# A written-out schedule changed: one state turned by a transfer, a new order and coarser pieces at the end

## The chip, the cores and the metric

The kernel runs on one core of one Trainium2 chip. The metric is device microseconds for one launch. Engines are called as in the profile: PE (matrix multiplications), PEld (its weight loads), DVE, ACT, POOL, and SP, which here only issues transfers. ACT and POOL issue transfers too.

## The reference, cut to what matters

For 8 batches and 8 heads, 512 tokens and 32 state rows of width 64 attend to each other in both directions. The results, 544 rows per batch with 512 columns, go through three products whose maximum is taken, and one more product:

```python
scores = scale * x @ state.T ; a = softmax(scores) ; xread = a @ state
scores2 = scale * state @ x.T ; a2 = softmax(scores2) ; sread = a2 @ x
x2 = concat([xread, sread], axis=2)            # (8, 8, 544, 64) -> (4352, 512)
h = maximum(maximum(x2 @ w1, x2 @ w2), x2 @ w3) # 512 -> 768
out = h @ w_out                                 # 768 -> 512, float32
```

## The kernel before

The kernel doesn't compute xread. For each batch it forms G = state times w1, w2 and w3 (`g_slice`, `g_run`), and layer 1 multiplies the turned weights aT by G (`layer1`, line 477). Layer 1 is done in six parts of 128 of the 768 columns; each part m fills three PSUM banks, one for each of the three weight matrices. ACT copies the first bank out (`max_first`, line 492), DVE takes the maximum with the second (`max_second`, 497) and with the third (`max_third`, 505). Layer 2 (`layer2`, 514) takes the 512 tokens of a batch in four groups j of 128 and accumulates over the six parts; ACT or DVE copies each result to `osb` (526), and a store sends it out. The 32 state rows of all 8 batches together make one more block "s" with 256 rows: layer 1 from `atp` and the weights (`layer1_states`), layer 2 in two groups.

At the end of the program, layer 2 of batch 7 and of block s is cut by columns: `layer2_part` (l2p, 532), `layer2_part_out` (l2pc, 537) and `store_part` (sop, 541 and 543) compute, copy and store the columns c0 to c1 of a group. `store_states` (sos, 556) stores a whole group of block s.

The states come in four tiles k, each for the batches 2k and 2k+1; state tile 3 serves batches 6 and 7. `states_cast` makes it bfloat16, `states_turn` (stt) turns it by four PE transposes (line 261), and `states_place` (stp, 271) spreads it into the block-diagonal tile `bd` by two copies. `states_turn_dma` (std, 265) is there too, unused: it turns a tile by one transfer that SP issues. The tokens of batches 2 to 7 are turned by transfers as well (`x_turn_dma`, xtd, 291), and so are the attention weights (`a_turn_dma`, atd, 366) and the state readings (`sread_turn`, srt, 410, placed by `sread_place`, ap, 415).

There is no scheduler. The string PLAN is a list of steps, performed in that order; each step puts its instructions at the end of its engine's queue, and engines run their queues in order, each waiting on semaphores for what it needs. The last letter of a step names the engine that copies (D, A, P) or the queue that issues a transfer (S, A, P). The strings BANKS, PAIRS and PLACES say which PSUM bank and which buffer each step takes. POOL multiplies the attention weights (`weights`, wt, 349), pads the tokens (`pad`, 375), and issues the loads of tokens (206, 201) and most stores (548).

The last steps are `hold` (one multiplication, line 591, and one DVE copy of it, 593) and `vl`: all engines read a flag (583) and branch (674) over a repeat of the work that is needed only if sums ran out of range. It isn't taken here. After it come the instructions with which the program ends (739).

Of the kernel before, what the change touches and what calls it, by code (L numbers as in the profile page):

```python
# [15 lines left out]


PLAN = """
    lst 0 A; lxu 0 0 S; zero; clr 0; clr 1; clr 2; clr 3; warm; lxg 0 1; busy 1; xones 1; ident; busy 1;
    lxg 1 0; busy 1; busy 1; stc 0 D; busy 1; busy 1; busy 1; busy 1; busy 1; lxg 1 1; stt 0; busy 1; busy 1;  # L20
    cxu 0 0 D; xt 0 0; stp 0 A; busy 1; xt 0 1; lw 0 2 1; lw 0 1 0; xtc 0 0 D; sc 0 0; xones 0; lw 0 2 2;
    xtc 0 1 D; busy 1; busy 1; sc 0 1; xt 1 0; ex 0 0; ex 0 1; lw 1 3 0; sum 0 0; sum 0 1; xtc 1 0 A; busy 1;
    busy 1; xt 1 1; sc 1 0; xtc 1 1 D; ex 1 0; busy 1; busy 1; sc 1 1; lw 2 3 2; wt 0 1 D; lw 2 3 1; lw 3 4 0;
# [11 lines left out]
    so 0 0 2 P; lx 4; m0 1 5; l2 0 2; ma 1 5; mb 1 5; stp 3 A; l2c 0 2 A; l2 1 0; gq 2 1024 1280; gr 3 0 512;
    gr 3 1792 2304; l2c 1 0 D; grc 3 1792 2304 D; gqc 2 1024 1280 A; grc 3 0 512 A; atd 2; sr 2; l2 1 1; srs 2;
    sc 3 -; l1 2 0; m0 2 0; ex 3 -; l2c 1 1 D; l2 1 3; ma 2 0; gq 3 1024 1280; so 0 2 4 P; gqc 3 1024 1280 A;
    l2c 1 3 A; gr 3 512 1024; gr 3 1280 1792; mb 2 0; sum 3 -; wt 3 - P; atd 3; xtd 4; srt 0; sr 3; srs 3;
    l1 2 1; m0 2 1; ma 2 1; l1 2 2; m0 2 2; mb 2 1; ma 2 2; l1 2 3; m0 2 3; mb 2 2; ma 2 3; l1 2 5; m0 2 5;
    mb 2 3; l2 1 2; grc 3 1280 1792 A; grc 3 512 1024 A; ma 2 5; mb 2 5; l2c 1 2 D; l1 2 4; so 1 2 4 P; m0 2 4;  # L40
    ma 2 4; lx 5; mb 2 4; so 1 0 2 P; pad 4; gr 4 1792 2304; gr 4 0 512; grc 4 1792 2304 AD; l2 2 0; l2 2 1;
    grc 4 0 512 D; l2c 2 0 A; l1 3 0; m0 3 0; sc 4 -; ex 4 -; xtd 5; l2c 2 1 D; l2 2 3; ma 3 0; gq 4 1024 1280;
    gr 4 1280 1792; gr 4 512 1024; mb 3 0; sr 4; gqc 4 1024 1280 A; sum 4 -; srs 4; l2c 2 3 A; l1 3 1; m0 3 1;
    ma 3 1; l1 3 2; m0 3 2; mb 3 1; ma 3 2; l1 3 3; m0 3 3; mb 3 2; ma 3 3; l1 3 5; wt 4 - P; m0 3 5; mb 3 3;
    l2 2 2; grc 4 1280 1792 A; grc 4 512 1024 A; ma 3 5; mb 3 5; l2c 2 2 D; l1 3 4; so 2 2 4 P; m0 3 4; ma 3 4;
    lx 6; mb 3 4; atd 4; srt 1; ap 0 A; so 2 0 2 P; pad 5; gr 5 1792 2304; gr 5 0 512; grc 5 1792 2304 AD;
    l2 3 0; l2 3 1; grc 5 0 512 D; l2c 3 0 A; l1 4 0; m0 4 0; sc 5 -; ex 5 -; xtd 6; l2c 3 1 D; l2 3 3; ma 4 0;
    gq 5 1024 1280; gr 5 1280 1792; gr 5 512 1024; mb 4 0; sr 5; gqc 5 1024 1280 A; sum 5 -; srs 5; l2c 3 3 A;
    l1 4 1; m0 4 1; ma 4 1; l1 4 2; m0 4 2; mb 4 1; ma 4 2; l1 4 3; m0 4 3; mb 4 2; ma 4 3; l1 4 5; wt 5 - P;
    m0 4 5; mb 4 3; l2 3 2; grc 5 1280 1792 A; grc 5 512 1024 A; ma 4 5; mb 4 5; l2c 3 2 D; l1 4 4; so 3 2 4 P;  # L50
    m0 4 4; ma 4 4; lx 7; mb 4 4; atd 5; srt 2; ap 1 A; so 3 0 2 P; pad 6; gr 6 1792 2304; gr 6 0 512;
    grc 6 1792 2304 AD; l2 4 0; l2 4 1; grc 6 0 512 D; l2c 4 0 A; l1 5 0; m0 5 0; sc 6 -; ex 6 -; xtd 7;
    l2c 4 1 D; l2 4 3; ma 5 0; gq 6 1024 1280; gr 6 1280 1792; gr 6 512 1024; mb 5 0; sr 6; gqc 6 1024 1280 A;
    sum 6 -; srs 6; l2c 4 3 A; l1 5 1; m0 5 1; ma 5 1; l1 5 2; m0 5 2; mb 5 1; ma 5 2; l1 5 3; m0 5 3; mb 5 2;
    ma 5 3; l1 5 5; wt 6 - P; m0 5 5; mb 5 3; l2 4 2; grc 6 1280 1792 A; grc 6 512 1024 A; ma 5 5; mb 5 5;
    l2c 4 2 D; l1 5 4; so 4 2 4 P; m0 5 4; ma 5 4; mb 5 4; atd 6; srt 3; ap 2 A; so 4 0 2 P; pad 7;
    gr 7 1792 2304; gr 7 0 512; grc 7 1792 2304 AD; l2 5 0; l2 5 1; grc 7 0 512 D; l2c 5 0 A; l1 6 0; m0 6 0;
    sc 7 -; ex 7 -; l2c 5 1 D; l2 5 3; ma 6 0; gq 7 1024 1280; gr 7 1280 1792; gr 7 512 1024; mb 6 0; sr 7;
    gqc 7 1024 1280 A; sum 7 -; srs 7; l2c 5 3 A; l1 6 1; m0 6 1; ma 6 1; l1 6 2; m0 6 2; mb 6 1; ma 6 2;
    l1 6 3; m0 6 3; mb 6 2; srt 4; ma 6 3; l1 6 5; wt 7 - P; m0 6 5; mb 6 3; l2 5 2; grc 7 1280 1792 A;  # L60
    grc 7 512 1024 A; ma 6 5; mb 6 5; l2c 5 2 D; l1 6 4; so 5 2 4 P; m0 6 4; ma 6 4; mb 6 4; atd 7; ap 3 A;
    ap 4 A; so 5 0 2 P; srt 6; l1 7 0; srt 7; m0 7 0; l2 6 0; ap 7 D; srt 5; ma 7 0; mb 7 0; l1 7 2; m0 7 2;
    ap 6 A; l2c 6 0 D; ma 7 2; l1 7 3; m0 7 3; ap 5 A; mb 7 2; ma 7 3; l1 7 4; m0 7 4; l2 6 1; l2c 6 1 A;
    ma 7 4; mb 7 4; l1s 0; m0 s 0; l2 6 2; l2c 6 2 A; look; ma s 0; mb s 0; so 6 2 3 S; mb 7 3; l1 7 1; m0 7 1;
    ma 7 1; l1s 2; m0 s 2; mb 7 1; ma s 2; l1 7 5; m0 7 5; mb s 2; ma 7 5; l1s 1; m0 s 1; ma s 1; so 6 0 1 S;
    mb 7 5; l1s 5; m0 s 5; l2p 7 2 384 512; ma s 5; mb s 1; mb s 5; l1s 3; m0 s 3; l2pc 7 2 384 512 A;
    l2p 7 0 384 512; l2p 7 3 256 512; sop 7 2 384 512 P; ma s 3; l2p 7 2 128 384; mb s 3; l2p 7 0 0 128;
    l2pc 7 0 0 128 A; l2pc 7 3 256 512 D; l2p 7 1 0 128; l2pc 7 0 384 512 D; l2p 7 3 0 256; flag;
    l2pc 7 1 0 128 A; l2pc 7 2 128 384 A; l1s 4; m0 s 4; l2 6 3; sop 7 0 0 128 P; ma s 4; sop 7 0 384 512 P;
    mb s 4; l2p s 0 256 512; so 6 1 2 P; l2 s 1; sop 7 3 256 512 A; l2c 6 3 D; l2p 7 2 0 128; sop 7 1 0 128 S;  # L70
    so 6 3 4 A; l2pc 7 3 0 256 D; l2p s 0 0 256; l2pc s 0 256 512 D; sop s 0 256 512 A; l2pc 7 2 0 128 A;
    l2p 7 1 128 384; sop 7 2 0 128 A; l2p 7 0 256 384; l2pc s 0 0 256 A; l2pc 7 1 128 384 A; l2c s 1 D;
# [671 lines left out]
```

## Time and profile before

| | us |
|---|---|
| median of 3 runs | 152.14 (152.1 to 152.29) |
| span of the profiled execution | 150.5 |
| last matrix multiplication of the work ends in it | 146.95 |
| PE busy | 145.1 (96% of the span) |
| DVE, ACT, POOL busy | 118.0, 83.2, 56.1 |

The granted TensorE clock is 1.000 in the profiled execution. The profile does not give that execution's own device time; the median of the runs is 1.64 us over its span. Queue rows (SPq, POOLq, ACTq) stand for what an engine's sequencer does: it issues transfers, waits, branches. They are not counted as busy. Times of PE in the chain of waits are cut at the next step's start, those of the timeline are not.

### The profile page before, as it was taken

What the parts mean: (1) busy time and instruction counts of PE and PEld (TensorE: products, weight loads), DVE (VectorE), ACT (ScalarE), POOL (GpSimd) and SP (SyncE); (2) the same over time, 40 slices, a digit from 0 to 9 for tenths busy, and PEclk for the clock granted to TensorE, in tenths of its full rate; (3) what the DMA queues carried; (4) which work ended last, traced back from release to release, by engine and by line L of the source; (5) the groups of instructions that cost most, each with busy time, mean ns of one, the idle gap of its engine ahead of it and who ended that gap; (6) DMA issues with size and microseconds to landing.
All of it is one profiled execution on the core that took longest, in us unless ns stands there. A gap on an engine that the chain in (4) does not pass through costs nothing.

```text
span 150.5 us, 3618 instructions
## 1 busy us (share of the span) xinstructions
PE 145.1 (96%) x1422; PEld 72.8 (48%) x1422; DVE 118.0 (78%) x202; ACT 83.2 (55%) x144; POOL 56.1 (37%) x78
## 2 busy tenths in 40 slices
PE   6998999999999999999999999999999999999991
PEld 2556443335444443444344434443444446689770
DVE  6488788999967899789978997899789888674443
ACT  3366888965654574457546764676466653332220
POOL 6996911090392507350735064506250200001500
PEclk9999999999999999999999999999999999999999
DMA  4999999949647996998399839983303340300555
GB/s 121 195 188 189 206 230 198 196 97 139 124 97 171 235 182 189 108 209 178 145 102 216 183 139 90 231 183 131 157 4 78 121 175 7 139 0 17 190 199 167
DMA packets 39108, 22.29 MB, mean 148 GB/s; under 512 B 23072, under 2 KB 36896, under 8 KB 39088
## 3 DMA queue, kind: packets, MB, share of 16 engines
q0 software_dynamic: 15872, 13.96, 49.3%
q1 hardware_dynamic: 21632, 6.69, 22.8%
q10 hardware_dynamic: 1584, 1.38, 3.2%
q8 instruction: 12, 0.20, 0.6%
q14 instruction: 8, 0.07, 0.2%
HBM read 15.20 MB, written 8.91 MB: 160 GB/s over the span
## 4 chain that ended last, share of the span: by engine, by line
PE 88%; DMA 5%; POOL 3%; issue 1%; DVE 1%; ACT 1%; POOLq 0%
PE pw L477 47%; PE po L514 25%; PE pg L427 6%; DMA w<-in_moe_w_dram 5%; PE po L532 4%; PE ps L305 2%; PE psr L391 2%; POOL w L217 1%; POOL x L206 1%; PE pgh L427 1%; ACT G L444 1%; PE pt L261 1%; DVE held L593 0%; PE idle L591 0%; PE pat L358 0%
## 5 line engine op out<-in xcount | busy, mean ns | idle before, releaser
L477 PE MATMUL pw<-aT,G 128*128 128x512 bf16 x288 | 66.7, 379 | 0.0
L492 ACT CAST t<-pw 128x512 bf16<-128x512 f32 (+1 forms) x54 | 30.5, 564 | 27.3 <-PE pw L477 26.4
L497 DVE TENSOR_TENSOR t<-t,pw 128x512 bf16<-128x512 bf16 (+1 forms) x54 | 35.3, 654 | 11.1 <-ACT t L492 8.9
L477 PEld LDWEIGHTS <-G 128*128 128x128 bf16 x288 | 27.1, 98 | 32.8 <-issue 2.1
L514 PE MATMUL po<-wout,ht 128*128 128x512 bf16 x168 | 39.7, 379 | 0.0
L505 DVE TENSOR_TENSOR ht<-t,pw 128x512 bf16<-128x512 bf16 x48 | 32.9, 686 | 4.5
L349 POOL TENSOR_TENSOR a<-e,rden 128x1024 bf16<-128x1024 bf16 (+1 forms) x9 | 14.6, 1622 | 27.2 <-ACT osb L526 11.1
L514 PEld LDWEIGHTS <-ht 128*128 128x128 bf16 x168 | 15.4, 98 | 19.0 <-issue 1.7
L548 POOL DMA_DIRECT2D out_dram<-osb x13 | 7.4, 571 | 27.5 <-ACT t L492 27.5
L466 ACT CAST G<-pg 128x1024 bf16<-128x1024 f32 (+1 forms) x17 | 14.7, 895 | 2.1 <-PE pg L427 2.1
L526 ACT COPY osb<-po 128x512 f32<-128x512 f32 x15 | 8.9, 592 | 9.1 <-PE po L514 9.1
L526 DVE COPY osb<-po 128x512 f32<-128x512 f32 x14 | 9.6, 688 | 3.9 <-PE po L514 3.8
L375 POOL COPY xp<-x 128x1024 bf16<-128x1024 bf16 x12 | 12.3, 1059 | 0.0
L313 ACT ACTIVATE e<-ps 128x1024 bf16<-128x1024 f32 (+1 forms) x10 | 8.5, 854 | 6.7 <-PE ps L305 6.7
L466 DVE CAST G<-pg 128x1024 bf16<-128x1024 f32 (+1 forms) x12 | 11.6, 995 | 0.0
L342 DVE TENSOR_REDUCE seen<-e 128x32 f32<-128x1024 bf16 (+1 forms) x10 | 10.0, 997 | 1.7 <-ACT e L313 1.7
L427 PE MATMUL pg<-w,bd 64*32 64x512 bf16 (+1 forms) x288 | 10.7, 362 | 0.4 <-DMA w<-in_moe_w_dram 0.2
L444 ACT CAST G<-pg 128x768 bf16<-128x768 f32 x10 | 8.0, 810 | 2.7 <-PE pg L427 2.5
L543 POOL DMA_DIRECT2D out_dram<-osb x4 | 2.2, 544 | 19.4 <-ACT osb L537 19.4
L249 PE MATMUL idle<-zero 128*128 128x512 bf16 x18 | 7.4, 506 | 1.8 <-DVE zero L225 1.3
L477 PE MATMUL pw<-atp,w 128*128 128x256 bf16 x72 | 8.7, 272 | 0.0
L217 POOL DMA_DIRECT2D w<-in_moe_w_dram x10 | 7.7, 782 | 0.0
(70 smaller groups left out, 112.1 us busy)
## 6 DMA issues: line engine op xcount, KB each, us to landing
out_dram<-osb POOLq DMA_DIRECT2D x12, 512.0 KB, 3.7
x<-in_x_dram POOLq DMA_DIRECT2D x4, 512.0 KB, 7.2
x<-in_x_dram POOLq DMA_DIRECT2D x7, 256.0 KB, 5.8
w<-in_moe_w_dram POOLq DMA_DIRECT2D x4, 256.0 KB, 7.5
w<-in_moe_w_dram POOLq DMA_DIRECT2D x2, 384.0 KB, 7.5
wout<-in_moe_w_out_dram POOLq DMA_DIRECT2D x1, 768.0 KB, 12.0
out_dram<-osb SPq DMA_DIRECT2D x3, 256.0 KB, 2.4
stf<-in_state_dram ACTq DMA_DIRECT2D x4, 128.0 KB, 5.3
```

The lines of the kernel that those rows point to most:

```text
L342: nc.vector.reduce_sum(out=den, in_=parity(e[b], g), axis=AX.X)
L349: times[c](out=parity(a[b], g).rearrange("p j g s n -> p j (g s) n"), in0=parity(e[b], g).rearrange("p j g s n -> p j (g s) n"), in1=rdens ...
L375: nc.gpsimd.tensor_copy(out=xp[b][:, :, :, g * (D + 1):g * (D + 1) + D], in_=v[:, g])
L427: nc.tensor.matmul(p(s, g), bd(b, 2 * s + g)[64 * g:64 * g + 64, g, :], f(w_sb[64 * g:64 * g + 64, s]), start=True, stop=True, tile_positi ...
L444: copier[c[g]](out=G[b][:, g:h, :, m * 128:m * 128 + 128], in_=p[:, g:h, 0:384].rearrange("p g (i f) -> p g i f", i=3))
L466: copier[c[g]](out=v[:, g:h], in_=p[:, g:h, 0:c1 - c0])
L477: nc.tensor.matmul(pw[i][:, 0:n], lhs(i, k), rhs(k), start=(k == 0), stop=(k == nk - 1))
L492: nc.scalar.copy(out=t0s[b, m][:, 0:n], in_=open_ps["l", b, m][0][:, 0:n])
L497: nc.vector.tensor_max(t1s[b, m][:, 0:n], t0s.pop((b, m))[:, 0:n], open_ps["l", b, m][1][:, 0:n])
L505: nc.vector.tensor_max(ht[b][:, m, :], t1s.pop((b, m))[:, 0:n], open_ps.pop(("l", b, m))[2][:, 0:n])
L514: nc.tensor.matmul(p, ht[b][:, m, tokens(b, j)], wout_sb[:, m, :], start=(m == 0), stop=(m == NM - 1))
L526: copier[c[i]](out=o[:, j, i * w:i * w + w], in_=p[:, i * w:i * w + w])
```

## The change

Only the four strings change: no function is edited. In the first 60 us, `stt 3` (four PE transposes) goes, and `std 3` comes; its placement moves from ACT to POOL. Steps of batches 2, 3 and 4 change their order, and a few copies change between ACT and DVE. From batch 5 on the order stays, up to the last part of batch 6. There, batch 7's parts of layer 1 and block s's are done in another order, and layer 2 of the end is cut otherwise: `l2p` steps go from 14 to 8 (with the one whole group of block s 9 pieces, where there were 15), `sop` from 14 to 8, and batch 6 is stored in two transfers where it took four.

```diff
-    mb 0 4; sc 2 -; ex 2 -; grc 2 512 1024 D; stp 2 AD; stc 3 D; mb 1 4; l2 0 3; l2 0 0; l2c 0 3 A; l2c 0 0 A;
-    sum 2 -; l2 0 1; ones; pad 2; lxg 3 0; lxg 3 1; wt 2 - P; stt 3; xtd 3; l2c 0 1 A; l1 1 5; pad 3;
...
+    1024 1280; gr 3 0 512; gr 3 1792 2304; so 0 2 4 P; gqc 2 1024 1280 A; l2c 1 0 A; grc 3 0 512 DA; sr 2; grc 3
...
+    m0 3 0; sc 4 -; ex 4 -; xtd 5; std 3; l2c 2 1 D; l2 2 3;
...
-    l2p 7 1 384 512; l2p 7 0 128 256; sop 7 3 0 256 S; sop 7 2 128 384 P; l2pc 7 0 256 384 D; sop 7 1 128 384 A;
-    l2pc 7 1 384 512 D; sop 7 1 384 512 A; l2pc 7 0 128 256 D; sop 7 0 128 256 A; sos 1 S; sop s 0 0 256 S;
-    sop 7 0 256 384 S; hold; vl;
...
+    512 A; l2p 7 0 0 128; l2p 7 1 384 512; sop s 0 0 512 S; l2pc 7 1 0 384 D; sop 7 1 0 384 S; l2pc 7 1 384 512
+    A; l2pc 7 0 256 512 D; l2pc 7 0 0 128 D; sop 7 0 256 512 S; sop 7 1 384 512 A; sos 1 P; sop 7 0 0 128 S;
+    hold; vl;
```

The end of POOL's queue, before and after. The three DMA rows L543 and L548 that go are the last stores that POOL issued (three of batch 7, one of batch 6, one of batch 7); L556 is the whole group 1 of block s (`sos 1`); the L415 copy is `ap 5`.

```order
 L548 DMA out_dram<-osb 128x1024 x2
-L543 DMA out_dram<-osb 128x128 x3
-L548 DMA out_dram<-osb 128x512
-L543 DMA out_dram<-osb 128x256
+L415 COPY atp<-ats 128x4x32
+L543 DMA out_dram<-osb 128x512
+L556 DMA out_dram<-osb 32x4x512
 L583 TENSOR_LOAD flag
```

POOL now ends on two stores of 256 KB, `sop 7 3 0 512` and `sos 1`, instead of five of 64 to 256 KB.

What stands ahead of those two stores on ACT, as the change has it. The rows are ACT's copies of `l2p 7 0 128 256`, `l2p 7 3 0 512`, `l2 s 1` and `l2p s 0 0 512`, the store of group 2, and the last copy with its store.

```order
L492 CAST t_2319<-pw_2310 128x512
L537 COPY osb<-po 128x128
L537 COPY osb<-po 128x512
L526 COPY osb<-po 128x512
L537 COPY osb<-po 128x512
L543 DMA out_dram<-osb 128x512
L537 COPY osb<-po 128x128
L543 DMA out_dram<-osb 128x128
L583 TENSOR_LOAD flag
```

The copy of group 1 of block s (L526) was DVE's before and stood late in its queue; now it is ACT's, directly behind the copy that the other POOL store waits for.

SP's queue in the middle: x_86 and x_87 are the tokens of batches 4 and 5, the aT rows are `atd 2`, `atd 3` and `atd 4`, and stT is the new transfer of state tile 3.

```order
 L291 DMA_TRANSPOSE xT<-x_85 128x16x128
-L366 DMA_TRANSPOSE aT<-a 128x8x128 x2
+L366 DMA_TRANSPOSE aT<-a 128x8x128
+L410 DMA_TRANSPOSE ats<-sr 128x128
+L366 DMA_TRANSPOSE aT<-a 128x8x128
 L291 DMA_TRANSPOSE xT<-x_86 128x16x128
-L410 DMA_TRANSPOSE ats<-sr 128x128
 L291 DMA_TRANSPOSE xT<-x_87 128x16x128
+L265 DMA_TRANSPOSE stT<-st 128x4x128
 L366 DMA_TRANSPOSE aT<-a 128x8x128
```

`srt 0` moves ahead of `atd 3`, and the new transfer stands between `xtd 5` and `atd 4`. On POOL the load of batch 5's tokens moves at the same time, from ahead of `pad 4` to behind it.

More of the change, by code (lines that the diff above doesn't have):

```diff
@@ L18 @@
 PLAN = """
[L19 to L23, printed above, removed]
@@ L34 @@
-    sum 2 -; l2 0 1; ones; pad 2; lxg 3 0; lxg 3 1; wt 2 - P; stt 3; xtd 3; l2c 0 1 A; l1 1 5; pad 3;
[L35 to L72, printed above, removed]
-    l2p 7 1 384 512; l2p 7 0 128 256; sop 7 3 0 256 S; sop 7 2 128 384 P; l2pc 7 0 256 384 D; sop 7 1 128 384 A;
@@ new lines @@
+    1 4; l2 0 3; stp 2 AD; stc 3 D; l2 0 0; l2c 0 3 A; l2c 0 0 A; ones; sum 2 -; lxg 3 0; lxg 3 1; wt 2 - P; xtd
+    3; l2 0 1; l2c 0 1 A; pad 3; l1 1 5; lx 4; m0 1 5; l2 0 2; ma 1 5; l2c 0 2 A; mb 1 5; l2 1 0; gq 2 1024
+    1280; gr 3 0 512; gr 3 1792 2304; so 0 2 4 P; gqc 2 1024 1280 A; l2c 1 0 A; grc 3 0 512 DA; sr 2; grc 3 1792
+    2304 D; l2 1 1; srs 2; atd 2; sc 3 -; srt 0; l1 2 0; m0 2 0; ex 3 -; l2c 1 1 D; so 0 0 2 P; l2 1 3; ma 2 0;
+    gr 3 1280 1792; gq 3 1024 1280; gqc 3 1024 1280 A; mb 2 0; gr 3 512 1024; sum 3 -; l2c 1 3 A; wt 3 - P; atd
@@ new lines @@
+    3; sr 3; l1 2 1; srs 3; m0 2 1; ma 2 1; l1 2 2; m0 2 2; mb 2 1; ma 2 2; l1 2 3; m0 2 3; mb 2 2; ma 2 3; l1 2
+    5; m0 2 5; mb 2 3; l2 1 2; grc 3 1280 1792 A; grc 3 512 1024 A; ma 2 5; mb 2 5; l2c 1 2 D; l1 2 4; m0 2 4;
+    ma 2 4; so 1 2 4 P; gr 4 1792 2304; mb 2 4; xtd 4; pad 4; grc 4 1792 2304 AD; gr 4 0 512; grc 4 0 512 D; l2
+    2 0; l2 2 1; lx 5; l2c 2 0 D; so 1 0 2 P; l1 3 0; m0 3 0; sc 4 -; ex 4 -; xtd 5; std 3; l2c 2 1 D; l2 2 3;
+    gq 4 1024 1280; ma 3 0; l2c 2 3 A; gr 4 1280 1792; gr 4 512 1024; mb 3 0; sr 4; gqc 4 1024 1280 A; sum 4 -;
@@ new lines @@
+    srs 4; l1 3 1; m0 3 1; ma 3 1; l1 3 2; m0 3 2; mb 3 1; ma 3 2; l1 3 3; m0 3 3; mb 3 2; ma 3 3; l1 3 5; wt 4
+    - P; m0 3 5; mb 3 3; l2 2 2; grc 4 1280 1792 A; grc 4 512 1024 A; ma 3 5; mb 3 5; l2c 2 2 D; l1 3 4; so 2 2
+    4 P; m0 3 4; ma 3 4; lx 6; mb 3 4; atd 4; srt 1; ap 0 A; so 2 0 2 P; pad 5; stp 3 P; gr 5 1792 2304; gr 5 0
+    512; grc 5 1792 2304 AD; l2 3 0; l2 3 1; grc 5 0 512 D; l2c 3 0 A; l1 4 0; m0 4 0; sc 5 -; ex 5 -; xtd 6;
+    l2c 3 1 D; l2 3 3; ma 4 0; gq 5 1024 1280; gr 5 1280 1792; gr 5 512 1024; mb 4 0; sr 5; gqc 5 1024 1280 A;
@@ new lines @@
+    sum 5 -; srs 5; l2c 3 3 A; l1 4 1; m0 4 1; ma 4 1; l1 4 2; m0 4 2; mb 4 1; ma 4 2; l1 4 3; m0 4 3; mb 4 2;
+    ma 4 3; l1 4 5; wt 5 - P; m0 4 5; mb 4 3; l2 3 2; grc 5 1280 1792 A; grc 5 512 1024 A; ma 4 5; mb 4 5; l2c 3
+    2 D; l1 4 4; so 3 2 4 P; m0 4 4; ma 4 4; lx 7; mb 4 4; atd 5; srt 2; ap 1 A; so 3 0 2 P; pad 6; gr 6 1792
+    2304; gr 6 0 512; grc 6 1792 2304 AD; l2 4 0; l2 4 1; grc 6 0 512 D; l2c 4 0 A; l1 5 0; m0 5 0; sc 6 -; ex 6
+    -; xtd 7; l2c 4 1 D; l2 4 3; ma 5 0; gq 6 1024 1280; gr 6 1280 1792; gr 6 512 1024; mb 5 0; sr 6; gqc 6 1024
@@ new lines @@
+    1280 A; sum 6 -; srs 6; l2c 4 3 A; l1 5 1; m0 5 1; ma 5 1; l1 5 2; m0 5 2; mb 5 1; ma 5 2; l1 5 3; m0 5 3;
+    mb 5 2; ma 5 3; l1 5 5; wt 6 - P; m0 5 5; mb 5 3; l2 4 2; grc 6 1280 1792 A; grc 6 512 1024 A; ma 5 5; mb 5
+    5; l2c 4 2 D; l1 5 4; so 4 2 4 P; m0 5 4; ma 5 4; mb 5 4; atd 6; srt 3; ap 2 A; so 4 0 2 P; pad 7; gr 7 1792
+    2304; gr 7 0 512; grc 7 1792 2304 AD; l2 5 0; l2 5 1; grc 7 0 512 D; l2c 5 0 A; l1 6 0; m0 6 0; sc 7 -; ex 7
+    -; l2c 5 1 D; l2 5 3; ma 6 0; gq 7 1024 1280; gr 7 1280 1792; gr 7 512 1024; mb 6 0; sr 7; gqc 7 1024 1280
@@ new lines @@
+    A; sum 7 -; srs 7; l2c 5 3 A; l1 6 1; m0 6 1; ma 6 1; l1 6 2; m0 6 2; mb 6 1; ma 6 2; l1 6 3; m0 6 3; mb 6
+    2; srt 4; ma 6 3; l1 6 5; wt 7 - P; m0 6 5; mb 6 3; l2 5 2; grc 7 1280 1792 A; grc 7 512 1024 A; ma 6 5; mb
+    6 5; l2c 5 2 D; l1 6 4; so 5 2 4 P; m0 6 4; ma 6 4; mb 6 4; atd 7; ap 3 A; ap 4 A; so 5 0 2 P; srt 6; l1 7
+    3; m0 7 3; ma 7 3; srt 7; mb 7 3; srt 5; l2 6 0; ap 6 A; l2c 6 0 A; l1 7 2; m0 7 2; ap 7 D; ma 7 2; mb 7 2;
+    l2 6 3; l1 7 4; l2c 6 3 D; ap 5 P; m0 7 4; ma 7 4; l1s 2; m0 s 2; mb 7 4; ma s 2; l1s 1; m0 s 1; ma s 1; mb
```

48 lines of the change are left out of this document (28 added, 20 removed), and 3 rows, old and new, of the table BANKS.

## The prediction

> **What bounds the kernel now.** I read the page's busy times, then the chain of waits in order of time.
>
> ```profile
> span 150.5 us, 3618 instructions
> 38.64 0.22 PE pt L261 x4
> 38.86 1.29 PE pw L477 x6
> ...
> 75.68 1.29 PE pw L477 x6
> ...
> 135.09 0.33 PE po L532 x6
> 135.43 1.31 PE pw L477 x12
> 136.74 2.97 PE po L532 x36
> ...
> 141.04 1.29 PE po L514 x6
> 142.34 0.66 PE po L532 x6
> 143.00 1.29 PE po L514 x6
> 144.29 2.67 PE po L532 x36
> 146.95 0.02 issue
> 146.98 0.30 DVE osb L537
> ```
>
> The reader is to see that one PE piece follows the other without a gap until 146.95. PE work that goes away there is time, if nothing new makes PE wait. But the span goes on for 3.5 us behind PE, and the chain doesn't say what ends it. So I read, line by line, the queue rows of the branch (674) and of the program's end (739), and the last transfers (issues with their time to landing, for windows around them).
>
> ```profile
> L674 POOLq EVENT_SEMAPHORE  x5: 17/42/43, 142.1 to 145.3; - x5
> L674 POOLq INC_SWDGE_SEM  x1: 967/967/967, 145.4 to 145.4; - x1
> L739 POOLq DRAIN  x3: 46/109/3247, 146.4 to 150.2; - x3
> L739 SPq DRAIN  x3: 7/7/13, 149.3 to 149.9; - x3
> L739 POOLq EVENT_SEMAPHORE  x4: 17/17/17, 149.7 to 150.4; - x4
> ```
>
> ```profile
> 140.91 0.54 POOL L543 DMA_DIRECT2D out_dram<-osb  x1
> out_dram<-osb POOLq DMA_DIRECT2D x1, 128.0 KB, 4.3
> 146.37 1.43 ACTq L543 DMA_DIRECT2D out_dram<-osb  x3
> out_dram<-osb ACTq DMA_DIRECT2D x3, 64.0 KB, 1.8
> ```
>
> Two chains end the program. **SP's**: the last of ACT's three stores is issued at about 147.4 (their 1.43 us end at 147.8, one issue is some 0.4), lands 1.8 later at 149.2, and SP is through its waits at 149.3. **POOL's**: its last store is issued at 140.91 and lands 4.3 later, at 145.2. POOL waits for that (its waits run to 145.3), then takes 0.97 for INC_SWDGE_SEM and 3.25 for the DRAIN that starts at 146.4, and so gets to 149.6. The joint end starts at 149.7, right behind POOL and 0.4 behind SP. So POOL's chain ends last, by a little: from its last landing, 0.2 + 0.97 + 3.25 = 4.4 us to 149.6, and 0.85 more to 150.5.
>
> **The change part by part.**
>
> *Transposes of state tile 3.* Four PE transposes leave the chain: 0.22 us (38.64). PE then comes 0.22 earlier to `l1 1 5`, whose first bank ACT must have emptied before `l2 0 2` may take it.
>
> ```profile
> 38.68 0.59 ACT L526 COPY osb<-po 128x512 f32<-128x512 f32 x1 [0.71 <-PE po L514]
> 39.33 0.59 ACT L492 CAST t<-pw 128x512 bf16<-128x512 f32 x1
> ```
>
> ACT's cast starts 0.06 us behind the copy since it waits for PE; if PE comes earlier, it follows the copy at once and ends at 39.26 + 0.59 = 39.85 at the latest. PE wants the bank at 38.86 + 1.29 - 0.22 = 39.93 by the chain's times, some 0.1 to 0.2 earlier by the timeline's. So up to 0.1 may be lost again. I count 0.2 of the 0.22; bounds 0 and 0.22.
>
> *The transfer in its place, and its placement.* `std 3` stands in SP's queue ahead of `atd 4`, which `l1 4 0` needs at 75.68. At the same time the load of batch 5's tokens goes behind `pad 4`.
>
> ```profile
> 57.94 0.91 POOL L201 DMA_DIRECT2D x<-in_x_dram  x1
> 59.42 2.05 POOL L375 COPY xp<-x 128x1024 bf16<-128x1024 bf16 x2
> x<-in_x_dram POOLq DMA_DIRECT2D x4, 512.0 KB, 7.2
> 65.24 3.47 SPq L291 DMA_TRANSPOSE xT<-x  x1
> 68.80 1.26 SPq L366 DMA_TRANSPOSE aT<-a  x1
> aT<-a SPq DMA_TRANSPOSE x6, 2.9
> ```
>
> Now the load comes about 2.1 us later, at 60.0; it lands at 67.2, `xtd 5` takes 3.5 of SP until 70.7, the state's transfer, half as large as an aT, at most 1.3 until 72.0, and aT of batch 4, 2.9 us from issue to landing, is there at 74.9. PE wants it at 75.5. I cost it at nothing; the cover is the 0.6 us that are left (3.9 before). The two copies into `bd`, of 512 elements a row, fall to POOL, for which the trace has none of this form; two of its padding copies, 1024 each, take 2.05, so I bound both by 0 and 2.1. They stand ahead of `wt 5`; POOL is idle for up to 3.8 us ahead of a `wt`, and `bd` is first read by `gr 6`, a batch later. Nothing.
>
> ```profile
> POOL a L349 <- ACT osb L526: 11.1, 3, 3.8
> ```
>
> *Batches 2 to 4 in another order, copies between ACT and DVE.* PE's row order is nearly the same; `wt 2` waits for the same sums. DVE gets 0.69 more where `l2c 2 0` comes to it, ACT as much less. Bounds: 0.1 lost where a bank comes free just in time, 0.1 gained. Nothing.
>
> *PE at the end.* The columns are the same, cut into fewer pieces. 128 columns take 0.33 in a piece alone, 512 take 1.29, 0.324 per 128. The runs of 1152 and 1024 columns took 2.97 and 2.67, where 2.91 and 2.59 would follow: 0.14 for 12 pieces. About half the pieces go: 0.07. DVE might fall behind in the new order:
>
> ```profile
> L497 DVE TENSOR_TENSOR t<-t,pw 128x512 bf16<-128x512 bf16 (+1 forms) x54 | 35.3, 654 | 11.1 <-ACT t L492 8.9 <-PE pw L477 2.0
> L505 DVE TENSOR_TENSOR ht<-t,pw 128x512 bf16<-128x512 bf16 x48 | 32.9, 686 | 4.5
> ```
>
> An l1 of 1.29 us brings DVE 0.65 + 0.69 = 1.34 us. Each one that is left stands next to a layer-2 group that ACT copies or to state parts of half the columns, where DVE catches up, so I count no new stall; bound 0.3 lost. PE then ends at 146.95 - 0.20 - 0.07 = 146.7.
>
> *The stores.* Behind `l2 s 1` PE does 2560 columns, 20 x 0.324 = 6.5; so it ends at 140.2, and `l2p 7 3 0 512`, 640 columns on, at 141.8. ACT copies that (0.59, to 142.4) and then group 1 of block s (0.59, to 143.0).
>
> ```profile
> 136.17 0.27 ACT L537 COPY osb<-po 128x128 f32<-128x128 f32 x1
> 136.74 0.55 POOL L543 DMA_DIRECT2D out_dram<-osb  x1 [17.34 <-ACT osb L537]
> L526 ACT COPY osb<-po 128x512 f32<-128x512 f32 x15 | 8.9, 592 | 9.1 <-PE po L514 9.1
> out_dram<-osb POOLq DMA_DIRECT2D x1, 64.0 KB, 2.0
> out_dram<-osb SPq DMA_DIRECT2D x1, 256.0 KB, 2.5
> out_dram<-osb POOLq DMA_DIRECT2D x1, 512.0 KB, 2.9
> out_dram<-osb POOLq DMA_DIRECT2D x1, 256.0 KB, 4.5
> out_dram<-osb ACTq DMA_DIRECT2D x1, 128.0 KB, 4.0
> out_dram<-osb POOLq DMA_DIRECT2D x1, 64.0 KB, 4.1
> ```
>
> POOL issues 0.3 behind the copy that it waits for (136.44 to 136.74) and takes 0.55 for an issue: `sop 7 3` at 142.7, `sos 1` at 143.3. When does it land? Two bounds: 2.0 us (64 KB from POOL) and 4.5 (256 KB from POOL at 140.4; what was issued beside it, 64 KB from POOL and 128 KB from ACT, took 4.1 and 4.0). Nearest are the same store from SP, 2.5, and 512 KB from POOL with nothing beside it, 2.9. I take 2.7: 146.0. Before it was 145.2. So POOL's chain moves by +0.8: 146.0 + 4.4 + 0.85 = 151.3 for the span.
>
> The Trainium skill, in "DMA: Bandwidth & Descriptors", section "Anatomy of one DMA — SWDGE (gpsimd) path", gives about 2.0 us and bytes / 436e3 us for a transfer of this queue. By it the store would land 2.6 us behind its issue, an estimate from the page, and the sum would be 0.1 less.
>
> *SP's chain* gets shorter: PE ends 0.27 earlier, and the last store is no longer the third of a row on one queue: DVE's last copy is for the piece before PE's last, and the last two stores go out on two queues. I take 0.4 (bounds 0.27 and 0.6): the last store at 147.0 instead of 147.4, the end of the chain at 148.9. That is worth nothing as long as POOL ends at 150.4.
>
> **Sum.** Span 150.5 + 0.8 = 151.3. The median lies 1.64 over the profiled span; so 152.14 + 0.8 = 152.9.
>
> **Rivals.**
>
> *POOL's tail isn't a fixed cost.* INC_SWDGE_SEM and the DRAIN stand in the trace once, and a wait could be in them that ends with the others, since POOL is done only 0.3 behind SP. Against it: the other DRAINs in the rows above last 0.007 to 0.109 us, this one follows an instruction that stands in the end only once, POOL has no transfer under way, and nothing lands within the 0.4 us before its end. If it's elastic, SP's chain decides and takes the 0.4 along: span 150.1, time 151.75, faster. It decides if POOL's tail shrinks by 1.5 us or more.
>
> The Trainium skill ("VectorE: DVE Perf Modes", section "The DRAIN you can't avoid") says that the DRAINs of a program's start and end are constant, about 12 ns, on all engines. By that rule POOL would be through at 146.4 and this rival's time would come; the trace doesn't agree, with 3247 ns in one of POOL's three.
>
> *The gain is eaten, and the store lands early.* If `sos 1` lands within 2.0 to 2.2 us, POOL's chain moves by 0.1 to 0.3 only: 152.2 to 152.4, no change that could be told.
>
> *SP is late for batch 4.* If the late load and the state's transfer together cost more than the 0.6 us of cover, PE stands still at `l1 4 0`. Everything behind moves, POOL's tail included. At a load of 8 us (0.8 more than now) that is 0.2 more, and 153.1.
>
> *The transposes weren't time.* If the 0.22 is lost again at a bank, all of the end moves 0.2 later: 153.1 with POOL's tail, 152.0 with an elastic one.
>
> **How the numbers follow.** A measurement of this kernel can tell 0.2%, 0.3 us, from no change. POOL's tail with the later store: 0.58. Elastic tail: 0.25, nearly all of it faster. Store lands early: 0.10. Late for batch 4, in whatever tail: 0.07. Slower: most of 0.58, and 0.03 to 0.05 of the last: 0.60. Faster: 0.26. Within: 0.14. The likeliest one's own range is from a landing after 2.3 us (+0.4: 152.5) to one after 3.6 us (+1.7: 153.8); the range with the elastic tail begins at 151.6. Time 152.9, range 151.6 to 153.8.
>
> **What would show it.** Right: the POOL row INC_SWDGE_SEM of 674 starts near 146.2 instead of 145.4, its DRAIN again takes near 3.2 us and ends behind SP's last DRAIN by more than a microsecond, PE's last piece ends at 146.6 to 146.8, the first piece behind 38.6 is layer 1. Wrong: the DRAIN gets shorter while its start comes later (elastic tail), a gap of PE near 75 (late aT), PE's last piece not earlier than 146.9, or a last POOL store that lands before 145.5.

## The result: 1.6% slower, three times the loss that was forecast

The changed kernel takes 154.75 us (median of 6 runs, 153.87 to 155.63), the kernel before 152.21 beside it (152.1 to 152.4): 1.016 times as long, 95% interval 1.0125 to 1.0196. The forecast was 152.9 in a range of 151.6 to 153.8. The direction was right, the size was not: +0.8 forecast, +2.5 measured. One run of a1 below took 171.07 us at a granted clock of 0.856, and the ratio of a1 leaves it out.

The chain of waits of the changed kernel, its last pieces (start, length, what):

```profile
core 0 of [0], span 152.1 us
...
142.80 3.63 PE po L532 x30
146.43 0.02 issue
```

PE's last piece ends at 146.43, and 5.7 us follow where the kernel before has 3.5 (146.95 to 150.5). So PE doesn't make the loss; the program's end does. The queue rows of the branch (674) and of the end (739), each with its shortest, median and longest duration in ns and its first and last start:

```profile
L674 POOLq EVENT_SEMAPHORE  x5: 17/43/2312, 144.6 to 147.2; - x5
L674 POOLq INC_SWDGE_SEM  x1: 907/907/907, 147.3 to 147.3; - x1
```

```profile
L739 POOLq DRAIN  x3: 46/109/3002, 148.2 to 151.8; - x3
L739 SPq DRAIN  x3: 7/7/13, 149.9 to 151.5; - x3
```

POOL waits 2.3 us for its last transfer, until 147.1, and then takes 0.91 and 3.00: it is through at 151.24, 1.4 behind SP's first DRAIN (149.85). That is the chain of the forecast. What it waits for is `sos 1`; first the row of its issue in the timeline, then the landing in the view of line 556:

```profile
142.95 0.57 POOL L556 DMA_DIRECT2D out_dram<-osb  x1
```

```profile
DMA to landing us min/median/max: 4.1/4.1/4.1
```

4.1 us, where 2.7 was forecast. By the trace's landing events 15 of its 16 parts were there after 2.42 to 2.58 us, the last one after 4.10. In the window from 144.6 to 145.0 the transfer queues show one packet that is no data:

```profile
q8 instruction: 1, 0.02, 14.6%
```

It starts at 144.62 and moves 16 KB of instructions; such a transfer, by which an engine gets its next instructions, is called a **fetch** below. The four late stores of the kernel before (4.0 to 4.5 us) look the same: the POOL stores issued at 140.38 and 140.91 had 15 parts down within 2.54 and 2.58 us and the last after 4.48 and 4.26, with such a packet at 141.41. Its row, in the window from 141 to 143 of the kernel before:

```profile
q8 instruction: 1, 0.02, 4.5%
```

In the middle nothing was lost, as forecast: the state's transfer and aT of batch 4 follow `xtd 5` on SP, the latter is issued at 70.47 and lands at 73.20 (forecast 72.0 and 74.9; the load of batch 5's tokens landed at 65.87, not at 67.2), and PE comes to `l1 4 0` at 75.00 without a gap. SP's rows of the timeline, then the chain:

```profile
65.94 3.11 SPq L291 DMA_TRANSPOSE xT<-x  x1
69.10 1.26 SPq L265 DMA_TRANSPOSE stT<-st  x1
70.47 1.24 SPq L366 DMA_TRANSPOSE aT<-a  x1
```

```profile
72.30 2.70 PE po L514 x12
75.00 1.29 PE pw L477 x6
```

Near the end of the program a new stall appeared. The chain of the changed kernel at the first part of batch 7, `l1 7 3`, and of the kernel before at its first, `l1 7 0`:

```profile
116.21 0.45 PE pw L477 x2
116.65 0.02 issue
116.67 0.59 ACT t L492
117.27 0.02 issue
117.29 0.70 DVE t L497
117.99 0.04 issue
118.03 1.02 PE pw L477 x4
```

```profile
116.88 2.59 PE pw L477 x12
```

Before, 12 multiplications in a row took 2.59; now the same 12, from 116.21 to 119.06, take 2.85, since PE waits for ACT and DVE to empty a bank of `l1 6 4`. Every kernel of this study with the new end has this stall in its chain, and none with the old end.

### The profile page after: what moved, and what is told of

Read it like the earlier page. It is cut to its first block, busy times and chain, and to the rows that moved or that the text cites. A ratio compares the mean times of both kernels' runs of the same rounds, so it can differ in the third digit from the quotient of the medians.

```text
span 152.1 us, 3520 instructions
## 1 busy us (share of the span) xinstructions
PE 144.4 (95%) x1382; PEld 69.9 (46%) x1382; DVE 117.8 (77%) x199; ACT 81.4 (54%) x139; POOL 57.1 (38%) x78
## 4 chain that ended last, share of the span: by engine, by line
PE 86%; DMA 5%; POOL 2%; issue 1%; ACT 1%; DVE 1%; POOLq 0%
PE pw L477 46%; PE po L514 25%; PE pg L427 6%; DMA w<-in_moe_w_dram 5%; PE po L532 4%; PE ps L305 2%; PE psr L391 2%; POOL w L217 1%; POOL x L206 1%; PE pgh L427 1%; ACT G L444 1%; DVE t L497 0%; DVE held L593 0%; ACT t L492 0%; PE pt L261 0%
## 5 line engine op out<-in xcount | busy, mean ns | idle before, releaser
L548 POOL DMA_DIRECT2D out_dram<-osb x12 | 6.8, 569 | 27.0 <-ACT t L492 21.5
L466 ACT CAST G<-pg 128x1024 bf16<-128x1024 f32 (+1 forms) x17 | 14.2, 871 | 2.1 <-PE pg L427 2.1
L466 DVE CAST G<-pg 128x1024 bf16<-128x1024 f32 (+1 forms) x13 | 12.2, 973 | 1.8 <-PE pg L427 1.8
L526 ACT COPY osb<-po 128x512 f32<-128x512 f32 x16 | 9.5, 592 | 7.5 <-PE po L514 7.5
L526 DVE COPY osb<-po 128x512 f32<-128x512 f32 x13 | 8.8, 687 | 0.9 <-PE po L514 0.9
L543 POOL DMA_DIRECT2D out_dram<-osb x1 | 0.5, 545 | 23.2 <-ACT osb L537 23.2
L249 PE MATMUL idle<-zero 128*128 128x512 bf16 x18 | 6.9, 472 | 1.7 <-DVE zero L225 1.3
L477 PEld LDWEIGHTS <-w 128*128 128x128 bf16 x72 | 7.0, 98 | 1.5
```

The source lines that it names most:

```text
L466: copier[c[g]](out=v[:, g:h], in_=p[:, g:h, 0:c1 - c0])
L477: nc.tensor.matmul(pw[i][:, 0:n], lhs(i, k), rhs(k), start=(k == 0), stop=(k == nk - 1))
L526: copier[c[i]](out=o[:, j, i * w:i * w + w], in_=p[:, i * w:i * w + w])
```

## The experiments

The theory to test, A: the end is POOL's, from the landing of its last store, and the fetch of instructions makes that landing late. Two rivals: B, the new order and the larger pieces are slow on whatever queue; C, the loss is in the middle. Each run is compared with runs of the kernel before on the same chip, whose medians were 151.98 to 152.35. One measure is free of what the head and PE do in one execution: the time in the profile from the end of PE's last piece to the end of the span. It is called **the end** below; 3.5 us before, 5.7 in the changed kernel.

### Each part alone, and the whole again

e3 joins the plan of the change up to `mb 6 4` with the end of before, e4 the plan of before with the end of the change:

```diff
 e3:  ... l1 6 4; so 5 2 4 P; m0 6 4; ma 6 4; mb 6 4;          (as changed)
      atd 7; ap 3 A; ap 4 A; so 5 0 2 P; srt 6; l1 7 0; ...    (as before)
 e4:  the other way round
```

> The first part of the change alone: state tile 3 turned by a transfer and the new order of batches 2 to 4, with the end of the kernel before from atd 7 on. Theory A: 151.9 to 152.2 (0 to 0.2 faster than before), since the four transposes are 0.22 us of PE and the end is POOL's, with the landing of its last store. Rival C (the transfer or the late load of batch 5's tokens costs in the middle): 0.3 or more slower than before.

> The second part alone: the middle of the kernel before, and from atd 7 on the end of the changed one. Theories A and B: 153.5 to 155, the whole of the loss. Rival C: within 0.5 us of before.

> The changed kernel once more, unedited. Its profiled execution (153.87) was the fastest of six; the median was 154.75. Theory A with two more collisions: an execution near the median has POOL's tail later (sos 1 landing after more than 4.1 us), or the aT of batch 2 held by a fetch (landing 4.3 to 4.5 instead of 2.7, PE 0.8 to 1.1 later from 44.7 on). If neither, something else makes the other 0.9 us.

Measured: e3 154.75, 1.015 times before (1.012 to 1.019); e4 154.89, 1.017 (1.012 to 1.023); e12 154.4, 1.016 (1.012 to 1.020). e4 and e12 are theory A again: ends of 6.1 and 5.6 us, `sos 1` landing after 4.5 and 4.0, with fetches at 144.3 and 144.9. e12's aT of batch 2 came after 2.73, so the second collision that its expectation names was not in it. But e3 was a miss for all theories: it is as slow as the whole change, and although it changes only the first part, its loss sits at the end of the program. Its rows of the branch and of the end:

```profile
L674 DVEq COMPARE_BRANCH  x1: 84/84/84, 148.5 to 148.5; - x1
L674 DVEq EVENT_SEMAPHORE  x1: 21/21/21, 151.7 to 151.7; - x1
```

```profile
L739 SPq EVENT_SEMAPHORE  x14: 17/28/3345, 147.8 to 152.7; - x14
```

DVE stands 3.1 us behind its branch, and SP waits 3.3 us for DVE. In the kernel before DVE goes on 0.5 behind the branch. Up to there e3 had won 0.1 us: from the first layer-1 piece to PE's last piece 131.1 us, against 131.2 before and in the changed kernel, and 131.4 in e4.

e8 is e3 with six tiny DVE writes more in the head:

```diff
-        nc.vector.memset(bds[k], 0.0)
+        [nc.vector.memset(v, 0.0) for v in [bds[k]] + [bds[k][:, 0, 0, 0, 0:1]] * (6 * (k == 3))]
```

> The kernel of e3_middle_alone (first part of the change alone, which came out at 154.75) with six tiny DVE writes (one column each) added in the head. In e3 DVE stood 3.08 us behind its branch at 148.53 where it stands 0.48 in the kernel before, and SP waited 3.3 us for it. Theory: that stall depends on where DVE's instruction stream lies when the branch comes, so six more instructions ahead of it take it away: 151.9 to 152.3, as was expected of e3. If the stall comes from the first part's own work (a late copy or load): it stays at 154.5 or more, with 3 us behind DVE's branch.

Measured: 151.87 against 152.14, ratio 0.9993 (0.9968 to 1.0017), and the stall is gone:

```profile
L674 DVEq COMPARE_BRANCH  x1: 84/84/84, 147.8 to 147.8; - x1
L674 DVEq EVENT_SEMAPHORE  x1: 21/21/21, 148.4 to 148.4; - x1
```

So the first part costs nothing, as forecast, and rival C falls. The stall goes with the number of DVE's instructions: all three kernels of this study whose trace has 325 of them had it (e3, k2, k3: 3.06 to 3.31 us), none with 320, 321, 324 or 331 had. That the place of the instructions decides is argued from this and from e8. What happens in those 3 us no run shows: in e3 three packets of instructions come behind the branch, the last is done at 150.3, and DVE stands for 1.4 us more in which the traced transfers are still; the kernel before has three such packets there, too, and no stall. The Trainium skill, in "Runtime: NRT & Kernel Launch", section "Instruction fetch mechanics", says that a taken branch to a place outside the pages at hand must wait for a fetch; a stall of 3.1 us behind a branch fits that, but 1.4 of it have no fetch beside them.

### The two stores of POOL

e1 takes both from POOL, a1 only `sos 1`; b1 puts `sos 1` alone on POOL in the kernel before:

```diff
 e1:
-sop 7 3 0 512 P; ... sos 1 P;
+sop 7 3 0 512 S; sos 1 S; ...
 a1:
-sop 7 3 0 512 P; ... sos 1 P;
+sop 7 3 0 512 P; sos 1 S; ...
 b1, in the kernel before:
-sos 1 S;
+sos 1 P;
```

> The changed kernel with its last two POOL stores (sop 7 3 and sos 1) issued by SP instead, sos 1 directly behind sop 7 3; nothing else. Theory A (POOL's tail ends the program: last landing of a POOL store, then about 3.9 to 4.2 us of INC_SWDGE_SEM and DRAIN, then 0.85): POOL is done early, SP's chain ends last at about 149.9 as it does in the changed kernel, span 150.5 to 150.8, time 152.1 to 152.6, 2 us faster than the changed kernel's 154.75. Theory B (the order and the larger pieces at the end are slow by themselves, whichever queue issues): stays at 154 or more. If INC_SWDGE_SEM and DRAIN are a fixed cost, they last 0.9 and 3.0 to 3.3 us here too, only earlier; if the DRAIN is a wait for something that ends with the program, it ends with SP's again.

> The changed kernel with that one store, sos 1, issued by SP; sop 7 3 stays on POOL. Theory A: POOL's last landing is sop 7 3 (2.4 to 2.7 behind its issue at 142.4, so at 145.0), POOL is through at about 149.3, and SP's chain, 0.7 late by the fetch, ends at about 150.0 as in e1: 4.2 to 4.3 us from PE's last piece to the end, as e1's 152.9. If both POOL stores are needed for the loss of the changed kernel or the fetch now holds sop 7 3: 4.5 to 5.7, 153.3 to 154.5.

> The kernel before with one letter changed: sos 1 issued by POOL instead of SP. Theory A: POOL issues it at about 145.1, it lands 2.5 to 2.8 later (147.6 to 147.9; the fetch at 141.4 is past), INC_SWDGE_SEM and DRAIN take 4.2, 0.85 more: from the end of PE's last piece to the end of the span 5.9 to 6.2 us instead of 3.5, time 2.3 to 2.7 slower than before. If POOL's tail were elastic: within 0.3 of before.

Measured: e1 152.9 (152.1 to 152.6 expected), 1.0045 times before (1.0019 to 1.0072); a1 153.21, 1.0062 (1.0034 to 1.0089); b1 153.58, 1.0091 (1.0061 to 1.0121). e1 takes 1.8 us of the loss away (1.016 to 1.0045): theory B falls. The end is 4.2 us, SP's. POOL's rows in e1:

```profile
L674 POOLq INC_SWDGE_SEM  x1: 867/867/867, 145.1 to 145.1; - x1
```

```profile
L739 POOLq DRAIN  x3: 46/109/2839, 146.0 to 150.6; - x3
L739 SPq DRAIN  x3: 7/7/13, 150.0 to 150.3; - x3
```

POOL's DRAIN lasts 2.84 us here too and is over at 148.8, 1.2 before SP: it waits for nobody, so the rival of an elastic tail falls. The Trainium skill's statement that the DRAINs of a program's end are constant, about 12 ns, on all engines ("VectorE: DVE Perf Modes", section "The DRAIN you can't avoid") agrees with SP's 7 to 13 ns here, and not with POOL's 46 to 2839. a1 misses its 4.2 to 4.3 by little (4.5, where its expectation began the case that the loss needs both stores): POOL was through at 149.0, and SP's last stores took 2.7 to 3.3 us to land behind a fetch at 145.6.

b1 was a miss. Its end is 4.5, not 5.9 to 6.2, although `sos 1` landed even later than expected, at 149.3 instead of 147.6 to 147.9 (issued at 146.4 instead of 145.1, 2.9 us to land with no fetch near):

```profile
L674 POOLq INC_SWDGE_SEM  x1: 351/351/351, 149.4 to 149.4; - x1
```

```profile
L739 POOLq DRAIN  x3: 46/109/716, 149.8 to 151.4; - x3
```

0.35 and 0.72 us, where 0.97 and 3.25 stood before. SP's chain ended last here; why its last stores were late (2.9 to 3.4 us) the trace doesn't settle.

### What sets POOL's end

Over the profiles, POOL's long DRAIN, the first of its three, goes with the number of transfers that POOL issued in the whole program: 34 (e1) 2.84, 35 (a1) 2.92, 36 (changed) 3.00, 37 (e11) 3.08, 39 (before) 3.25. That is 0.0816 us each and 0.065 once. b1 has 40, and 0.72 is what that line gives for 8. k1 to k3 change the number, by cutting some of POOL's earlier stores in two:

```diff
 k1, in the changed kernel, for b = 2, 3, 4, 5; k2, in the kernel before, for b = 5:
-so b 0 2 P;
+so b 0 1 P; so b 1 2 P;
 k3, in the kernel before:
-so 5 2 4 P; ... so 5 0 2 P;
+so 5 2 3 P; so 5 3 4 P; ... so 5 0 1 P; so 5 1 2 P;
```

> The changed kernel (36 POOL transfers) with four earlier POOL stores (the first halves of batches 2 to 5) cut into two each, so that POOL issues 40. Theory N (the number sets POOL's end, and at 40 only 8 count, 0.35 and 0.72 us, as in b1): POOL is through 1.1 us behind its last landing instead of 3.9, at about 148.4, SP's chain ends last at 149.9, 4.2 us from PE's last piece to the end as in e1 instead of 5.6, time 152.8 to 153.2. Rival (b1 was short because its last store came behind the load of the flag, or because it was late): DRAIN 3.33, 0.4 later than the changed kernel, 154.5 to 155.2.

> The kernel before (39 POOL transfers) with the POOL store of the first half of batch 5 cut into two: 40. Theory N: INC_SWDGE_SEM 0.35 and DRAIN 0.72 instead of 0.97 and 3.25, POOL is through at about 146.5, SP's chain ends last: 0.3 to 0.4 less from PE's last piece to the end (3.1 to 3.2), time 0.2 to 0.4 faster than before. Rival: DRAIN 3.33, 0 to 0.1 slower.

> The kernel before with both POOL stores of batch 5 cut into two: 41 POOL transfers. Theory N: nine count, DRAIN 0.80 (0.72 + 0.08) and INC_SWDGE_SEM 0.37; time as with 40. If 40 is an exception: DRAIN 3.41.

The rows of k1 (40 transfers) and of k3 (41):

```profile
L674 POOLq INC_SWDGE_SEM  x1: 351/351/351, 148.4 to 148.4; - x1
```

```profile
L739 POOLq DRAIN  x3: 46/109/716, 148.8 to 151.0; - x3
```

```profile
L739 POOLq DRAIN  x3: 46/109/797, 144.8 to 152.2; - x3
```

0.716 and 0.797, within 2 ns of what the line gives for 8 and 9. k1 takes 153.14 us, 1.0070 times before (1.0043 to 1.0097), where the changed kernel has 1.016: four cuts of stores far from the end win 1.4 us. `sos 1` still landed late (3.9), but SP ended the program, with an end of 4.2. The price of the 40th transfer stands in k1's POOL rows of the timeline: it came 0.84 us behind the end of the 39th, though ACT had copied its data by 143.2. In k2 and k3 it came 0.71 and 0.74 behind.

```profile
143.03 0.54 POOL L543 DMA_DIRECT2D out_dram<-osb  x1 [22.70 <-ACT osb L537]
144.41 0.57 POOL L556 DMA_DIRECT2D out_dram<-osb  x1 [0.84 <-ACT osb L537]
```

k2 and k3 didn't become faster, against what was expected (154.8 and 154.38, 1.016 and 1.014): both have 325 DVE instructions and the 3 us stall of e3, which hides what POOL won.

### The fetch

Six runs move the fetch by more PE instructions in the head; that it moves with them shows that it is PE's. e2 adds 24 multiplications of one column to the changed kernel. The others cut each of the 18 that keep PE busy into two (e5: changed, e6: before, e7: e1) or four (e9: changed, e10: e1):

```diff
-        for _ in range(n):
-            nc.tensor.matmul(p, zero[:, 0:128], zero, start=True, stop=True)
+        for i in range(2 * n):
+            nc.tensor.matmul(p[:, i % 2 * 256:i % 2 * 256 + 256], zero[:, 0:128], zero[:, 0:256], ...)
```

> The changed kernel with 24 matmuls of one column added to the first step that keeps PE busy in the head, so that PE's next 16 KB fetch of instructions (at 144.6 in the changed kernel, beside the last stores) comes 48 PE instructions earlier in the program, at about 140.0. Theory A with the fetch (one of the 16 DMA engines is held by the fetch, and the part of sos 1 on it lands 1.7 us behind the other 15): sos 1 lands after 2.5 to 2.8 us, at 145.5 to 145.8, POOL's tail begins 1.3 earlier, time 152.4 to 153.4. If the late landing comes from the load of stores on the 16 engines and not from the fetch: sos 1 lands after 4 us again, 154 to 155.

> The changed kernel with each of the 18 matmuls that keep PE busy in the head cut into two of 256 columns: 36 more PE instructions for the same columns (18 matmuls, 18 weight loads), so that the 16 KB fetch at 144.6 comes at about 141.5, without the 1 to 2 us that the added work of the run e2_fetch_moved cost in the head. Theory A with the fetch: sos 1 lands after 2.5 to 2.8 us, POOL's INC_SWDGE_SEM starts at 145.6 to 146.0, span 150.5 to 150.9, time 152.3 to 152.7. If the late landing isn't the fetch's: 154 or more.

> The kernel before with the same cut of the 18 matmuls in the head, which moves its fetch from 141.4 to about 139.4, ahead of its last POOL stores. Theory A: the last POOL store (issued 140.9) lands after 2.0 to 2.4 us instead of 4.3, POOL is through at about 147.6, SP's chain (149.35) ends last: 0.2 to 0.4 faster than before. If POOL's tail didn't end the kernel before (an elastic tail, or SP's chain last in most executions): within 0.1%.

> The kernel of e1_stores_off_pool (no store by POOL at the end) with the same cut of the 18 matmuls in the head. In e1 the last stores took 2.5 to 2.65 us to land (1.7 to 1.8 for the same sizes in the kernel before) behind a fetch at 145.2. Theory A: with the fetch at about 142, they land after 1.7 to 1.9, SP's chain ends 0.7 earlier, span 150.0 to 150.3, time 151.8 to 152.1, 0.2 to 0.5 faster than before. If the fetch isn't what holds them: 152.9 as in e1.

> The changed kernel with each of the 18 matmuls that keep PE busy in the head cut into four of 128 columns: 108 more PE instructions for the same columns. In e5 the fetch at the end was out of the way (sos 1 landed after 2.58 us), but the earlier fetch at 44.8 held one engine of aT of batch 2 (4.51 us instead of 2.71) and PE stood 1.1 us. With 108 instructions the fetches come at about 41.9 (0.6 behind the issue of aT of batch 2, instead of 2.5) and 135.2, away from both. Theory A with the fetch: aT lands after 2.7, sos 1 after 2.6, span 150.6 to 150.9, time 152.3 to 152.7. If anything but the fetch delays these two transfers: 154 or more.

> The kernel of e1_stores_off_pool with the same cut into four. Theory A: no POOL tail, no fetch at the last stores (1.7 to 1.9 us to land, as they had in e7) and none at aT of batch 2 (which cost e7 1.1 us): span 149.9 to 150.2, time 151.6 to 152.0, faster than before by 0.1 to 0.5. Otherwise 152.9 as in e1.

At the end of the program the expectations held each time; the expected times came in none of the six, as told below the table. The landing of `sos 1` in e5 (view of line 556):

```profile
DMA to landing us min/median/max: 2.6/2.6/2.6
```

| the end, us | fetch at 144.6 to 145.2 | fetch at 137.8 to 142.4 |
|---|---|---|
| both stores on POOL | 5.7 (changed), 5.6 (e12) | 4.2 (e2), 4.2 (e5), 4.2 (e9) |
| both stores on SP | 4.2 (e1) | 3.5 (e7), 3.5 (e10) |

The fetch is worth 1.5 us with POOL's stores (`sos 1` lands after 2.6 instead of 4.1) and 0.7 without (SP's last stores after 1.8 to 1.9 instead of 2.5 to 2.65). POOL's stores cost 0.7 even without the fetch. Together that is all of the 2.2 us. In e6 the end of the kernel before went from 3.5 to 3.2, SP last: POOL's chain did end it, by 0.3.

But none of these kernels was fast: e2 154.86, e5 154.26, e7 153.27, e6 153.35, e9 154.4, e10 153.36, 1.008 to 1.017 times before. So the worth of the fetch is read from the ends in the profiles, one execution of each kernel, and no time shows it alone. With the fetch moved, something else was late. (In e2 the added multiplications also lengthen the head: its first layer-1 piece comes at 16.68, in the changed kernel at 15.16.) In e5 the chain shows it at aT of batch 2:

```profile
42.32 4.51 DMA aT<-a
46.83 0.04 issue
46.87 1.24 PE pw L477 x5
```

4.5 us from issue to landing, where it takes 2.7 in the changed kernel; again 15 parts were down after 2.59 to 2.70 and the last after 4.51, with a fetch at 44.8. PE lost 1.1 us there in e5, e6 and e7, and 0.8 in e2 (aT after 4.25). A fetch alone isn't enough: before, in the changed kernel and in a1 one starts as long behind the issue (2.46 to 2.50 us, in e5 2.49), and there the transfer wasn't late. What decides it no run shows. Over all 20 traces 139 transfers had their last part more than 0.8 us behind the 15th; in 135 of them a fetch on q8 began between 1 us before the issue and the landing. The same holds of 487 of the 1354 others. In e9 and e10 it was the head: PE stood 1.0 us for nothing that the profile shows (e9), or the weights landed after 8.4 us instead of 6.9 to 7.4 (e10). e9 and e10 had a fetch at 12.1, and in e10 15 parts of the weights were there after 7.4, but that it was the cause is only argued. The Trainium skill ("Runtime: NRT & Kernel Launch", section "Instruction fetch mechanics") says that fetches come in blocks of 16 KiB, 256 instructions, and that crossing a block is mostly hidden. The 16 KB agree. That it is hidden holds for PE here, whose last piece runs through the fetch at 144.62 without a gap, and not for the late transfers beside it.

### A version that beats both?

e11 is e8 with the last two POOL stores of the end on SP. c1 is e11 with two earlier stores of batch 6 on POOL instead of SP:

```diff
 e11:
-so 6 1 2 P; ... sop 7 2 128 384 P;
+so 6 1 2 S; ... sop 7 2 128 384 S;
 c1, also:
-so 6 2 3 S; ... so 6 0 1 S;
+so 6 2 3 P; ... so 6 0 1 P;
```

> The kernel of e8_middle_dve_shifted (first part of the change, end of the kernel before, DVE's branch without its stall) with the last two POOL stores of the end (so 6 1 2 and sop 7 2 128 384) issued by SP. In e8 POOL's DRAIN ended at 149.25 and SP's at 148.63. Theory A (POOL's tail binds before too): POOL's last store is then issued at 139.2, POOL is through by 146, SP's chain decides: 0.5 to 0.6 faster than e8, 151.1 to 151.4, 0.6 to 1.0 faster than before. If the tail is elastic or SP's chain moves along with the two more stores: as e8, 151.9.

> The kernel of e11 with two earlier stores of batch 6 (so 6 2 3 and so 6 0 1, at about 129) issued by POOL instead of SP, so that the semaphores of the last stores turn by two places. In e11 the last store to land (148.74) has a semaphore that SP waits for sixth from the end, and SP needs 0.06 us for each that follows: its DRAIN starts at 149.19, 0.45 behind; in e8 the last store's semaphore is the last in the row, and SP is through 0.09 behind it. Theory: with the row turned, SP is through 0.35 earlier than in e11: 3.1 to 3.3 us from PE's last piece to the end (3.56 in e11, 3.52 before), 151.6 to 151.9, 0.1 to 0.4 faster than before. Rival: POOL's two early stores move POOL's other work, or the end waits for something else: as e11.

Measured: e11 152.14 against 151.98, 1.0005 (0.9988 to 1.0023); c1 152.09 against 152.32, 1.0001 (0.9972 to 1.0030). In e11 POOL is through at 145.8, but the end is 3.6, not 3.2: SP's waits run through the semaphores in a fixed order, 0.06 us each, and six more waits stood behind that for the last store to land (148.74). c1 turned the row, and SP's DRAIN in its profile follows the last landing (148.63) at once:

```profile
L739 SPq DRAIN  x3: 7/7/13, 148.7 to 149.0; - x3
```

The end is 3.1 us, 0.4 less than before, as expected of c1. The time (151.6 to 151.9 expected; 151.1 to 151.4 of e11) shows nothing of it beyond the spread of the runs (151.41 to 153.33): no version here beats the kernel before, though e8, e11 and c1 equal it.

## Why the forecast was right and wrong

**Right.** POOL's chain ends both kernels (e6: by 0.3 us before; the changed one by 1.4). `sos 1` is issued 3.5 us ahead of the end of PE's last piece, 3.4 forecast. INC_SWDGE_SEM and DRAIN follow the landing, wait for nobody, and end more than 1 us behind SP. The transfer of state tile 3, the late load, the order of batches 2 to 4 and the placement on POOL (2.23 us for both copies, a little over the bound of 2.1) cost nothing. The rival of SP's lateness for batch 4 did not occur.

**The step that failed: "When does it land? ... I take 2.7".** It took 4.1, which is 1.4 us of the missing. 2.6 is what it takes without the fetch, so the 2.7 was right for a free way. The range ended at a landing after 3.6, below the 4.0 to 4.5 of the four late stores, and so the measured time lay outside it. The bound of 4.5 was read as an effect of the stores beside it; the row that would have told was there, one instruction packet in the window from 141 to 143 of the kernel before. In both traces it comes at nearly the same PE instruction (the 2748th record of PE before, the 2732nd now), and as the coarser pieces need fewer instructions, PE gets there later: 144.6 instead of 141.4, just where `sos 1` moves its data. Had I asked what the four late stores had in common and then counted instructions, 4.1 would have been the likelier of the two. The Trainium skill's figures for this queue ("DMA: Bandwidth & Descriptors", section "Anatomy of one DMA — SWDGE (gpsimd) path") gave an estimate of 2.6; the runs agree with it in e2, e5 and e9 (2.6, no fetch near), less in b1 (2.9, none near), and not where a fetch is near (3.9 to 4.5).

**"PE at the end", "I count no new stall; bound 0.3 lost".** The bound came true: 0.26 at `l1 7 3`. From the first layer-1 piece to PE's last piece both kernels take 131.2 us, so the forecast gain of 0.27 (0.20 and 0.07) is gone: the first part alone brought 0.1 (e3, e8), the end alone lost 0.2 (e4). That is 0.3 more. Of the transposes' 0.22 about 0.1 came out in e3 and e8, so the rival that they weren't time was half right.

**"from its last landing, 0.2 + 0.97 + 3.25 = 4.4 us", a fixed cost.** Right in kind, wrong in that it isn't constant: 0.08 us of DRAIN and 0.02 of INC_SWDGE_SEM for each transfer of POOL, so 0.3 less with 36 than with 39.

The sum: 0.8 + 1.4 + 0.3 - 0.3 = 2.2, the 2.2 by which the end grew in the profile (5.7 - 3.5), where PE's work is as long in both. The medians differ by 2.5; the other 0.3 I can't assign, and both profiled executions of the changed kernel (153.87, and 154.15 in e12) were faster than its median. The heads of single executions alone differ by more (PE's first work on the weights at 13.04 in the changed kernel's profile, 13.60 before, 13.41 in e12).

**The rivals.** The elastic tail, at 0.25, falls with e1 and c1 (DRAINs of 2.84 and 3.25 us that end 1 to 3 us before SP's). But POOL's end can be short, for another reason: at 40 transfers. "The store lands early" didn't happen; the landing was wrong to the other side.

## What to carry to other kernels

The last transfer of an engine is priced to its landing, and the landing by what else uses its way: look in the queue rows for instruction packets near the transfers that something waits for, ask when the next one comes, and give the late landing a term and a chance of its own if it falls there. A kernel that is tuned to the last microsecond has luck in it that any shift of instructions moves (a fetch onto another transfer, a stall at a branch), so one part of a change that tests slow may only have lost that luck: shift it by a few idle instructions before judging it. Stores that only POOL's end waits for belong on another queue, or early.
